# Scores of two heads as 64-row products, one copy of q, the second element's block means moved, and the first unit's q and k loaded in runs of tokens

## The chip, the cores and the metric

The kernel runs on one core of a Trainium2 chip. The metric is the device time of the whole program in microseconds, as a median of several runs. Five engines work side by side: TensorE (PE in the profile, with its weight loads as PEld), VectorE (DVE), ScalarE (ACT), GpSimd (POOL) and SyncE (SP), which issues all the DMA transfers here.

## The reference

The kernel computes an attention over 4 batch elements, 8 heads, 768 positions and 64 columns, and behind it a feed-forward part with weights 512 x 2048 and 2048 x 512. A query sees the keys that lie less than 16 positions away, and besides one summary key for each block of 32 positions (their maximum, column by column) with the mean of the block's values.

```python
k_sum = k.reshape(B, H, nb, block, D).max(axis=3)
v_sum = v.reshape(B, H, nb, block, D).mean(axis=3)
scores_l = scale * np.matmul(q, k.transpose(0, 1, 3, 2))
mask_l = np.abs(pos[:, None] - pos[None, :]) < window
scores_s = scale * np.einsum('bhsd,bhnd->bhsn', q, k_sum)
scores_s = scores_s + np.log(block)
...
a = np.exp(scores_all)
a = a / (np.sum(a, axis=-1, keepdims=True) + 1e-09)
return np.matmul(a, v_all).astype(np.float32)
...
h = x @ w_in
g = h - np.tanh(h)
return (g @ w_out).astype(np.float32)
```

All of it is in float32.

## The kernel before

The work is cut into 8 units, two halves of 384 tokens for each batch element. A unit has 4 pairs of heads, so there are 32 pairs in all; two pairs form a group with common loads. For a pair the steps are: the turns of q and k (`prep`: heads' columns onto partitions, 64 for each head of the pair), copies of them to SBUF (`q high`, `k high`), the block maxima put beside the keys (`top put`), the scores (`score`), the softmax (`min`, `exp`, `sum guard`, `inverse`, `normal`), the turns of the probabilities (`p turn`, `p out`) and the values (`value`). After its four pairs a unit goes through the feed-forward part, 16 chunks `f` of 128 hidden columns each, with products `in`, a pointwise part and products `out`.

A score product covers 64 queries of one head and 118 keys (94 neighbours and 24 block maxima). Its q operand has 128 rows, of which the other head's 64 are zeros; `qf` therefore holds two copies of q, one for each head, and `zeros` fills the unused halves once. Four products, 2 heads x 2 halves of the queries, make one tile of 128 queries, and 3 tiles a pair. The halves go to partitions 0 to 63 and 64 to 127 of a PSUM bank. From the second unit on, the scores of a pair are issued as one task behind the values of the pair before (`scores_and_values`).

Maxima and means of the blocks for the first two batch elements come from loads of their own (`load_part`, then `top_pair` for k and `sum_pair` and `place_v` for v); those for the third and fourth are made later by VectorE and GpSimd. The tables `TOPS` and `SUMS` say in which slot `j` of the program a pair's maxima and sums stand; the loads go into rings of buffers (`gt`, `gu`, `gv`, `gh`, `gl`) that the feed-forward part uses afterwards. The mean of a group is put into the value operand by two transfers (`put_mean`), issued after the sums.

The weights come in 32 loads of 512 KB (`convert`) through a ring of 3 buffers (`wraw`) and are rebuilt by ScalarE and VectorE (`w scale`, `w shift`, `w low`, `w sign`). The first unit's feed-forward part runs while they arrive, with whole float32 products; each weight is split into a high and a low part behind its first use, and later units use three products of these parts.

The order of the program isn't the order of the code. Every step is a task with a cost, and a planner (`Plan.schedule`) simulates the engines, gives each free engine the ready task with the highest level, and emits the tasks in that order. A level is the longest chain behind a task plus two table entries, `BIAS` (for one task) and `KB` (for a kind in a phase); `SL` says how long a step that two engines can do waits for its first engine. A change of any cost, table or dependency can move instructions anywhere. While TensorE has nothing to do in the first part, the planner fills in products on the identity (`keep_warm`), whose outputs nobody reads.

Every operation is issued through one helper, so that the profile gives one line, L72, for nearly all instructions; the tiles tell them apart. `pS`, `pX`, `pY` and `pH` are PSUM banks, `rawq`, `rawk` and `vw` the loaded rows, `wf` a whole weight, `wh` and `wl` its high and low part.

Of the kernel before, what the change touches and what calls it, by code (L numbers as in the profile page):

```python
# [10 lines left out]
F32 = mybir.dt.float32  # L11
# [13 lines left out]

PLAIN = 3
# [11 lines left out]

PREP = [0, 2, 6, 11]

TOPS = {0: [(0, 0)], 1: [(0, 2)], 3: [(0, 1)], 5: [(0, 3)], 9: [(1, 3)], 11: [(1, 2)], 13: [(1, 0)], 15: [(1, 1)]}
SUMS = {0: [(0, 0)], 1: [(0, 1), (1, 1)], 8: [(0, 2)], 9: [(0, 3)], 10: [(1, 0)], 11: [(1, 2)], 13: [(1, 3)]}

SIGNED = set()
# [60 lines left out]
class Plan:  # L105
# [56 lines left out]
    def schedule(self, idle):  # L162
# [49 lines left out]
        while total:  # L212
# [20 lines left out]
            if e == PE and idle is not None:  # L233
                cost, go = idle
                if now > free[PE]:
                    free[PE] = max(free[PE], min(now, getattr(tasks[0], "out", now) + self.SEEN[POOL]))
                while free[PE] < WARM and now - free[PE] > 2 * cost + 0.1:
                    d = Task()
                    d.after, d.order, d.behind = tasks[:1], (), ()
                    d.start, d.engine, d.go = free[PE], PE, go  # L240
                    d.out = free[PE] = clock.run(free[PE], cost)
                    done.append(d)
                now = max(now, free[PE])
# [57 lines left out]
def program(  # L301
# [129 lines left out]
    ident, mask, blk, ga, small = (made[n,] for n in ("ident", "mask", "blk", "ga", "small"))  # L431
# [65 lines left out]
    for j in range(2):  # L497
        zeros(j)
# [839 lines left out]
```

## Time and profile before

| | |
|---|---|
| median of the runs | 727.91 us (725.0 to 730.04) |
| the profiled execution | 722.92 us |
| its span | 721.2 us |
| mean granted TensorE clock | 0.991 |
| HBM read and written | 96.21 MB and 23.07 MB |

The profiled execution's own time is 1.7 us longer than the span between its first and last instruction, and 5.0 us shorter than the median. In a row of the profile "x24" is a number of instructions; a float32 product, other than a transpose, counts twice there, since it is carried out as two instructions. The mean of one instruction is longer than the distance from one to the next, because products overlap; a group's cost is therefore read from the start of the group to the start of what follows it.

### The profile page before, as it was taken

The numbers are of one execution on the slowest core, as the hardware profiler recorded it, in microseconds if no ns is written. First come the engines' busy times: TensorE is split into PE (matmuls) and PEld (weight loads), VectorE is DVE, ScalarE is ACT, GpSimd is POOL, SyncE is SP. The second block draws the span as 40 slices with busy tenths as digits, with TensorE's granted clock in tenths as the row PEclk, the third lists the DMA queues.
The fourth block names the chain that finished last, engine by engine and source line by source line (L and its number), as shares of the span: only waits on it lengthen the run. The fifth ranks groups of instructions, "written<-read, shape, count | busy, mean of one in ns | idle before, by whom it ended". The sixth has DMA issues, their size and how long they took to land.

```text
span 721.2 us, 14213 instructions
## 1 busy us (share of the span) xinstructions
PE 688.8 (96%) x4787; PEld 572.6 (79%) x4787; DVE 431.6 (60%) x1180; ACT 482.3 (67%) x1411; POOL 256.4 (36%) x394
## 2 busy tenths in 40 slices
PE   6898799999999998999999999999999999999995
PEld 5685455558888787889988878998998888999884
DVE  4567878986996645654766557554568533444241
ACT  3467577767789776775897577555669965334981
POOL 3011421131246617422457563433345531111440
PEclk9999899999999999999999999999999999999998
DMA  9989968965665677567465557566544323444101
GB/s 211 234 239 239 307 197 225 281 200 151 202 171 166 179 238 206 138 196 190 123 182 170 164 136 225 142 180 177 170 146 147 119 87 115 147 162 145 45 1 50
DMA packets 158002, 122.67 MB, mean 170 GB/s; under 512 B 94816, under 2 KB 123744, under 8 KB 157920
## 3 DMA queue, kind: packets, MB, share of 16 engines
q1 hardware_dynamic: 157920, 121.67, 58.4%
q8 instruction: 40, 0.66, 0.4%
q14 instruction: 42, 0.34, 0.1%
HBM read 96.21 MB, written 23.07 MB: 165 GB/s over the span
## 4 chain that ended last, share of the span: by engine, by line
PE 77%; DMA 9%; ACT 5%; DVE 3%; SPq 3%; POOL 2%; issue 1%; POOLq 0%; ACTq 0%; DVEq 0%
PE pY L72 34%; PE pH L72 31%; PE pS L72 7%; PE pX L72 5%; SPq L72 3%; DMA wraw<-in_moe_w_in_dram 2%; DMA wraw<-scr 1%; POOL gh L72 1%; ACT prob L72 1%; ACT gu L72 1%; DMA wraw<-in_moe_w_out_dram 1%; DMA gh<-in_v_dram 1%; ACT tmp L72 1%; DVE wf L72 1%; DVE tmp L72 1%
## 5 line engine op out<-in xcount | busy, mean ns | idle before, releaser
L72 PE MATMUL pY<-wf,gh 128*128 128x512 f32 x432 | 178.9, 443 | 5.2 <-POOL gh L72 5.2
L72 PE MATMUL pH<-wh,wraw 128*128 128x384 f32 x672 | 175.3, 342 | 1.3 <-DMA wraw<-scr 1.3
L72 PE MATMUL pY<-wh,gh 128*128 128x512 f32 x336 | 139.4, 415 | 0.0
L72 PE MATMUL pY<-wh,gl 128*128 128x512 f32 x336 | 132.8, 395 | 0.0
L72 PEld LDWEIGHTS pH<-wh,wraw 128*128 128x128 f32 x672 | 120.2, 188 | 9.6 <-DMA wraw<-scr 1.5
L72 POOL TENSOR_TENSOR gu<-gu,gt 128x384 f32<-128x384 f32 x59 | 61.4, 1041 | 185.8 <-ACT gu L72 161.5
L72 ACT ACTIVATE prob<-prob,stat 128x118 f32<-128x118 f32 x248 | 92.3, 384 | 21.3 <-DVE stat L72 20.9
L72 PEld LDWEIGHTS pY<-wf,gh 128*128 128x128 f32 x432 | 80.6, 190 | 30.4 <-issue 12.7
L72 PE MATMUL pH<-wf,wraw 128*128 128x384 f32 x309 | 104.1, 337 | 0.0
L72 PEld LDWEIGHTS pY<-wh,gl 128*128 128x128 f32 x336 | 63.2, 188 | 14.8
L72 PEld LDWEIGHTS pY<-wh,gh 128*128 128x128 f32 x336 | 63.4, 189 | 12.1 <-issue 2.3
L72 ACT ACTIVATE gu<-gu 128x384 f32<-128x384 f32 x128 | 66.9, 523 | 2.2
L72 PE MATMUL pH<-o,wf 128*128 128x384 f32 x188 | 65.3, 446 | 1.6 <-DVE wf L72 1.6
L72 PEld LDWEIGHTS pH<-wf,wraw 128*128 128x128 f32 x309 | 58.0, 188 | 0.0
L72 ACT ACTIVATE gh<-gu 128x384 fp32r<-128x384 f32 x67 | 34.8, 522 | 30.9 <-PE pY L72 21.6
L72 DVE COPY gv<-pH 128x384 f32<-128x384 f32 x50 | 27.9, 558 | 42.4 <-PE pH L72 42.4
L72 DVE CUSTOM_DVE_ANT_0 prob<-pS,mask 128x118 f32<-128x118 f32 x180 | 40.7, 273 | 20.7 <-PE pS L72 20.6
L72 PEld LDWEIGHTS pH<-o,wf 128*128 128x128 f32 x188 | 35.7, 193 | 20.5 <-issue 4.4
L72 ACT ACTIVATE gt<-gu 128x384 f32<-128x384 f32 x42 | 21.9, 523 | 37.1 <-DVE gu L72 36.9
L72 DVE TENSOR_TENSOR gl<-gu,gh 128x384 fp32r<-128x384 f32 x38 | 22.7, 596 | 39.6 <-ACT gh L72 35.7
L72 POOL TENSOR_TENSOR gl<-gu,gh 128x384 fp32r<-128x384 f32 x32 | 33.6, 1055 | 29.4 <-ACT gh L72 27.7
L72 POOL TENSOR_TENSOR gh<-gu,gt 128x384 f32<-128x384 f32 x15 | 23.3, 1555 | 57.3 <-ACT gu L72 33.9
(212 smaller groups left out, 1298.2 us busy)
## 6 DMA issues: line engine op xcount, KB each, us to landing
wraw<-scr SPq DMA_DIRECT2D x75, 512.0 KB
wraw<-in_moe_w_in_dram SPq DMA_DIRECT2D x16, 512.0 KB
wraw<-in_moe_w_out_dram SPq DMA_DIRECT2D x16, 512.0 KB
scr<-wraw SPq DMA_DIRECT2D x16, 512.0 KB
rawq<-in_q_dram SPq DMA_DIRECT2D x48, 128.0 KB
out_dram<-tmp SPq DMA_DIRECT2D x24, 256.0 KB
wraw<-scr SPq DMA_DIRECT2D x21, 256.0 KB
rawk<-in_k_dram SPq DMA_DIRECT2D x32, 128.0 KB
```

The lines of the kernel that those rows point to most:

```text
L72: return lambda *args, **kwargs: self._tc.keep_in_program_order(op(*args, **kwargs))
```

## The change

**Scores.** A product now has only the 64 rows of its head: head 0 uses rows 0 to 63 of `qf` and `kf`, head 1 rows 64 to 127. `qf` holds one copy of q, made by one copy of 128 rows; the zero fills are gone. The heads alternate in the innermost loop, and each head has a bank of its own for its three tiles.

**The second element's maxima and means.** They leave `TOPS` and `SUMS`. Their 16 loads stand in slots 16 and 26 now, into the places of the split weights `wh22` to `wh29`, and the sums, mean turns and maxima in slots 22 to 31, where the first unit's feed-forward part has begun.

**Runs of tokens.** For the first unit a partition of `rawq` takes 3 neighbouring tokens and one of `rawk` 4, in one transfer each and one of a single row, and the turns are products on the identity that write every third or fourth column. The v loads for the sums take 6 tokens of one head in each partition instead of 3 of two heads; the block matrix `blk` becomes 6 x 24 wide and lies in a weight's place. A sum has all 6 products of one head and then all 6 of the other.

**The planner.** `BIAS`, `KB` and `SL` have new numbers throughout, several costs are changed, and a filler product is followed by a pause of 0.1. The tables are left out here.

```diff
+RUNS = 1
+
...
-TOPS = {0: [(0, 0)], 1: [(0, 2)], 3: [(0, 1)], 5: [(0, 3)], 9: [(1, 3)], 11: [(1, 2)], 13: [(1, 0)], 15: [(1, 1)]}
-SUMS = {0: [(0, 0)], 1: [(0, 1), (1, 1)], 8: [(0, 2)], 9: [(0, 3)], 10: [(1, 0)], 11: [(1, 2)], 13: [(1, 3)]}
+TOPS = {0: [(0, 0)], 1: [(0, 2)], 3: [(0, 1)], 5: [(0, 3)]}
+SUMS = {0: [(0, 0)], 1: [(0, 1)], 8: [(0, 2)], 9: [(0, 3)]}
...
-                    d.out = free[PE] = clock.run(free[PE], cost)
+                    d.out = clock.run(free[PE], cost)
+                    free[PE] = d.out + 0.1
...
-    fixed(("blk",), [P, 3, NBH])
+    buf(("blk",), f"wh{2 * NF - 2}", [P, 6, NB])
...
-        buf(("qf", j), f"q{j}", [P, 2, U])
+        buf(("qf", j), f"q{j}", [P, 2 if j else 1, U])
...
-    RAWK = [(("rawk",), i) for i in range(4)]
+    RAWK = [(("rawk",), i) for i in range(5)]
...
+    def in_runs(u):
+
+        return u < RUNS
+
+    def by_runs(x, n):
+        return x.rearrange("p i h d -> p (i h d)").rearrange("p (h t d) -> p h t d", h=HG, t=n)
...
-    def zeros(j):
-        for a in range(2):
...
-            do("const", POOL, 0.75, lambda a=a, o=o: gpsimd.memset(at(("qf", j))[o:o + 64, a], 0.0), w=[(("qf", j), "zero%d" % a)])
-
-    for j in range(2):
-        zeros(j)
-    do("const", DVE, 0.2, lambda: vector.memset(rawk[0:79, 0], 0.0), w=[RAWK[0]])
-    do("const", DVE, 0.2, lambda: vector.memset(rawk[96:P, 3], 0.0), w=[RAWK[3]])
+    do("const", DVE, 0.6, lambda: vector.memset(rawk[0:32], 0.0), w=RAWK)
+    do("const", DVE, 0.6, lambda: vector.memset(rawk[96:P], 0.0), w=RAWK)
...
-                sync.dma_start(st.rearrange("r (a t d) -> r a t d", a=2, t=3), v[b, hs, ts].rearrange("a (r t) d -> r a t d", t=3))
+                sync.dma_start(st, v[b, 2 * p + h].rearrange("(r t) d -> r (t d)", t=6))
...
-            for h in range(2):
-                st = at(("v", b, p, h)).rearrange("r (a t d) -> r a t d", a=2, t=3)
-                for t in range(3):
-                    for a in range(2):
-                        tensor.matmul(at(ps)[D * a:D * (a + 1), NBH * h:NBH * (h + 1)], st[:, a, t], blk[:, t], start=t == 0, stop=t == 2)
...
+            for a in range(2):
+                st = at(("v", b, p, a)).rearrange("r (t d) -> r t d", t=6)
+                for t in range(6):
+                    tensor.matmul(at(ps)[D * a:D * (a + 1), :NB], st[:, t], at(("blk",))[:, t], start=t == 0, stop=t == 5)
...
+        def runs(keys, r0, r1, c0, c1):
+            n, s0 = c1 - c0, t0 - 79 + 4 * r0 + c0
+            src = k[b, hs, s0:s0 + (r1 - r0) * n].rearrange("h (r t) d -> r h (t d)", t=n)
...
+        if in_runs(u):
+            if u % 2 == 0:
+                runs(RAWK[:4], 20, 120, 0, 4)
+                runs(RAWK[4:], 19, 20, 3, 4)
+            else:
+                runs(RAWK[:4], 16, 115, 0, 4)
+                runs(RAWK[4:], 115, 116, 0, 3)
+            src = q[b, hs, t0:t0 + U].rearrange("h (r t) d -> r h (t d)", t=NT)
+            dma("q load", lambda: sync.dma_start(by_runs(rawq, NT).rearrange("r h t d -> r h (t d)"), src), P * HG * D * 4 * NT, 4 * D * NT, w=RAWQ)
+            return
...
+            if in_runs(u):
+                for t in range(n):
+                    for a in range(2):
+                        tensor.matmul(at(ps)[D * a:D * (a + 1), :P * n].rearrange("p (r t) -> p t r", t=n)[:, t], by_runs(raw, n)[:, hs.start + a, t], ident, start=True, stop=True)
+                return
...
-        do("q turn", PE, 0.285, lambda: transposes(pq, rawq, NT), r=[*RAWQ, IDENT], w=[(pq, 0)])
...
-        for a in range(2):
-            rows = slice(64 * a, 64 * a + 64)
-            either("q high", {ACT: 0.42, DVE: 0.5}, lambda e, a=a, rows=rows: copy(e, at(qf)[rows, a], at(pq)[rows, :U], -1.0 / math.sqrt(D)), r=[(pq, 0)], w=[(qf, a)])
+        do("q turn", PE, 0.68 if in_runs(u) else 0.285, lambda: transposes(pq, rawq, NT), r=[*RAWQ, IDENT], w=[(pq, 0)])
+        do("k turn", PE, 0.9 if in_runs(u) else 0.395, lambda: transposes(pk, rawk, 4), r=[*RAWK, IDENT], w=[(pk, 0)])
...
+        either("q high", {ACT: 0.42, DVE: 0.5}, lambda e: copy(e, at(qf)[:, 0], at(pq)[:, :U], -1.0 / math.sqrt(D)), r=[(pq, 0)], w=[(qf, 0)])
...
-        return [(("qf", n), x) for x in (0, 1, "zero0", "zero1")] + [(("kf", n), x) for x in (0, "sums0", "sums1")]
...
-    def score_of(u, p, i):
-        return ("s", u, p, i // 2), 2 * N2 * (i % 2)
+        return [(("qf", n), 0)] + [(("kf", n), x) for x in (0, "sums0", "sums1")]
...
+    def score_of(u, p, i, a):
+        return ("s", u, p, a), N2 * i
...
         for i in range(NT):
-            s, c = score_of(u, p, i)
-            for a in range(2):
-                for half in range(2):
+            for half in range(2):
+                for a in range(2):
+                    s, c = score_of(u, p, i, a)
                     k0 = KS * i + 64 + 64 * half
-                    tensor.matmul(at(s)[64 * half:64 * half + 64, c + N2 * a:c + N2 * (a + 1)], at(qf)[:, a, P * i + 64 * half:P * i + 64 * half + 64], at(kf)[:, k0:k0 + N2], start=True, stop=True)
+                    rows = slice(64 * a, 64 * a + 64)
+                    tensor.matmul(at(s)[64 * half:64 * half + 64, c:c + N2], at(qf)[rows, 0, P * i + 64 * half:P * i + 64 * half + 64], at(kf)[rows, k0:k0 + N2], start=True, stop=True)
...
-            place_v(1, (j - 23) // 8, "pS1")
+        if B > 1 and j in (16, 26):
+            for n, (kind, p1, h) in enumerate((kind, p1, h) for kind in "vk" for p1 in range(2) for h in range(2)):
+                load_part(kind, 1, p1 + (j - 16) // 5, h, f"wh{22 + n}")
+        if B > 1 and 22 <= j < 32 and (j - 22) % 6 < 4:
+            g, n = divmod(j - 22, 6)
+            if n < 2:
+                sum_pair(1, PG * g + n, "pH")
+                if n == 1:
+                    place_v(1, g, "pS1")
+            else:
+                top_pair(1, PG * g + n - 2, "pH")
```

What the change moves is seen in the order of instructions. A row stands for neighbouring instructions that read alike; names are those above, with a buffer's number behind them where there are several, and the sizes are the transfer's, or the product's weight columns and moving columns.

SyncE at the start of the program, before:

```order
L72 DMA gt<-in_k_dram 128x3x128 x2
L72 DMA rawk<-in_k_dram 128x4x64
L72 DMA rawq<-in_q_dram 128x4x64 x2
L72 DMA rawk<-in_k_dram 49x4x64
L72 DMA rawk<-in_k_dram 128x4x64
L72 DMA rawk<-in_k_dram 96x4x64
L72 DMA rawq<-in_q_dram 128x4x64
L72 DMA gv<-in_k_dram 128x3x128
L72 DMA gu<-in_v_dram 128x2x192 x2
```

Seven transfers bring the first group's q and k, with 64 elements a run. The same place now:

```order
L74 DMA gt<-in_k_dram 128x3x128 x2
L74 DMA gv<-in_k_dram 128x3x128
L74 DMA rawq<-in_q_dram 128x4x192
L74 DMA rawk<-in_k_dram 1x4x64
L74 DMA rawk<-in_k_dram 100x4x256
L74 DMA gu<-in_v_dram 128x384 x2
L74 DMA gu<-in_k_dram 128x3x128
L74 DMA gh<-in_v_dram 128x384
```

Three transfers do it, with 192 and 256 elements a run, and the v loads have 384 in one run.

SyncE around the second mean put of the first unit's second group (`vw<-mean`) and the weight loads (`wraw<-in_moe`), before:

```order
L72 DMA vw<-in_v_dram 96x4x64
L72 DMA vw<-mean 24x3x256
L72 DMA rawq<-in_q_dram 128x4x64
L72 DMA vw<-in_v_dram 64x4x64
L72 DMA rawq<-in_q_dram 128x4x64 x2
L72 DMA wraw<-in_moe_w_in_dram 128x4x256
L72 DMA wraw<-in_moe_w_out_dram 128x1024
L72 DMA wraw<-in_moe_w_in_dram 128x4x256
L72 DMA rawk<-in_k_dram 64x4x64
```

All loads for the second element's means are ahead of this place but one. Now:

```order
L74 DMA wh_581<-in_v_dram 128x384
L74 DMA wh_588<-in_v_dram 128x384
L74 DMA wh_597<-in_k_dram 128x3x128
L74 DMA wh_604<-in_k_dram 128x3x128
L74 DMA vw<-mean 24x3x256 x2
L74 DMA wh_627<-in_v_dram 128x384
L74 DMA wraw<-in_moe_w_in_dram 128x4x256
L74 DMA wraw<-in_moe_w_out_dram 128x1024
L74 DMA wraw<-in_moe_w_in_dram 128x4x256
L74 DMA rawq<-in_q_dram 128x4x64 x2
```

Those loads (`wh`) stand among the weights now; eight of the sixteen come behind these rows.

TensorE in the first unit's feed-forward part, around the scores of a pair of the second unit, before:

```order
L72 MATMUL pS_68<-ident,prob 118x128 x2
L72 MATMUL pH<-o_448,wf_1079 128x384
L72 MATMUL pH<-o_453,wf_1079 128x384
L72 MATMUL pH<-o_766,wf_1079 128x384
L72 MATMUL pH<-o_811,wf_1079 128x384
L72 MATMUL pX<-probT,vw 64x64 x12
L72 MATMUL pS_1138<-k_254,q_138 64x118 x8
L72 MATMUL pS_68<-k_254,q_138 64x118 x4
L72 MATMUL pH<-o_448,wf_1155 128x384
```

Values, then scores: eight products into one bank, four into the other. Now, with the sum of one pair of the second element (`pH<-wh_123`, where `wh_123` is the block matrix) ahead of it:

```order
L74 MATMUL pH<-o_697,wf_1094 128x384
L74 MATMUL pH<-wh_123,wh_811 64x24 x6
L74 MATMUL pH<-wh_123,wh_892 64x24 x6
L74 MATMUL pX<-probT,vw 64x64 x12
L74 MATMUL pS_1180<-k_287,q_254 64x118
L74 MATMUL pS_68<-k_287,q_254 64x118
...
L74 MATMUL pH<-o_406,wf_1193 128x384
```

The scores go to the two banks in turn, and a sum of the second element stands between the feed-forward products.

More of the change, by code (lines that the diff above doesn't have):

```diff
@@ L430, in program @@
     fixed(("small",), [P, 1])
-    ident, mask, blk, ga, small = (made[n,] for n in ("ident", "mask", "blk", "ga", "small"))
+    ident, mask, ga, small = (made[n,] for n in ("ident", "mask", "ga", "small"))
     def make_ident():
@@ L461, in program @@
     do("const", POOL, 2.3, make_mask, w=[MASK])
-    do("const", POOL, 0.7, make_blk, w=[BLK])
+    do("const", POOL, 1.2, make_blk, w=[BLK])
     do("const", DVE, 0.05, lambda: vector.memset(ga, GA), w=[GAK])
@@ L636, in load_part @@
     def load_part(kind, b, p, h, tag):
-        base = buf((kind, b, p, h), tag, [P, U], F32, RINGS[tag])
-        hs, ts = slice(2 * p, 2 * p + 2), slice(U * h, U * (h + 1))
+        base = buf((kind, b, p, h), tag, [P, U], F32, RINGS.get(tag, 1))
         def load():
@@ L657, in top_pair @@
                    r=[(st[a], 0)] if a else (), w=[(st[0], 0)])
-        do("top turn", PE, 0.325, lambda: [tensor.transpose(at(ps)[:, P * c:P * (c + 1)], at(st[0])[:, P * c:P * (c + 1)], ident) for c in range(3)],
+        do("top turn", PE, 0.42, lambda: [tensor.transpose(at(ps)[:, P * c:P * (c + 1)], at(st[0])[:, P * c:P * (c + 1)], ident) for c in range(3)],
            r=[(st[0], 0), IDENT], w=[(ps, 0)])
@@ L686, in go @@
                 tensor.matmul(at(ps)[:NB, P * pr:P * (pr + 1)], at(x)[:, pr], ident, start=True, stop=True)
-        do("mean turn", PE, 0.5, go, r=[(x, pr) for pr in range(PG)] + [IDENT], w=[(ps, 0)])
+        do("mean turn", PE, 0.55, go, r=[(x, pr) for pr in range(PG)] + [IDENT], w=[(ps, 0)])
         do("mean out", ACT, 0.28, lambda: scalar.activation(mean[32 * g:32 * g + NB], at(ps)[:NB, :HG * D], AF.Copy), r=[(ps, 0)], w=[MEAN[g]])
@@ L735, in go @@
                 tensor.matmul(at(ps)[:NB, D * hh:D * (hh + 1)], ident[:96, NB * hh:NB * (hh + 1)], at(acc)[:96], start=True, stop=True)
-        do("mean turn", PE, 0.44, go, r=[(acc, 0), IDENT], w=[(ps, 0)])
+        do("mean turn", PE, 0.55, go, r=[(acc, 0), IDENT], w=[(ps, 0)])
         do("mean out", ACT, 0.28, lambda: scalar.activation(mean[32 * g:32 * g + NB], at(ps)[:NB, :HG * D], AF.Copy, scale=1.0 / 32), r=[(ps, 0)], w=[MEAN[g]])
@@ L849, in scores_and_values @@
     def scores_and_values(now, before, tags, px_tag):
-        r, w, cost, parts = [], [], 0.25, []
+        r, w, cost, parts = [], [], 0.13, []
         if before is not None:
             px = bank(("px", *before), px_tag)
-            r, w, cost = r + value_keys(*before), w + [(px, i) for i in range(NT)], cost + 0.75
+            r, w, cost = r + value_keys(*before), w + [(px, i) for i in range(NT)], cost + 0.72
             parts.append(lambda: value(*before))
@@ L857, in scores_and_values @@
             banks = [bank(("s", u, p, n), tag) for n, tag in enumerate(tags)]
-            r, w, cost = r + score_keys(u, p), w + [(x, n) for x in banks for n in range(4)], cost + 1.23
+            r, w, cost = r + score_keys(u, p), w + [(x, n) for x in banks for n in range(NT)], cost + 0.6
             parts.append(lambda: score(*now))
@@ L865, in first @@
         def first(i, a):
[L866 to L867 removed]
+            s, c = score_of(u, p, i, a)
             m = 1 if u % 2 == 0 and i == 0 else 2 if u % 2 == 1 and i == NT - 1 else 0
@@ L887, in softmax @@
         for i, a in both:
-            s, _ = score_of(u, p, i)
-            do("min", DVE, 0.21, lambda i=i, a=a: first(i, a), r=[(s, 2 * (i % 2) + a), MASK], w=[(("pr", u, p, i), a), (st, 2 * i + a)])
+            s, _ = score_of(u, p, i, a)
+            do("min", DVE, 0.21, lambda i=i, a=a: first(i, a), r=[(s, i), MASK], w=[(("pr", u, p, i), a), (st, 2 * i + a)])
         for i, a in both:
```

23 lines of the change are left out of this document (10 added, 13 removed).

## The prediction

> **What bounds the kernel now.** I read the page first, for the span and for which engine fills it.
>
> ```profile
> span 721.2 us, 14213 instructions
> PE 688.8 (96%) x4787; PEld 572.6 (79%) x4787; DVE 431.6 (60%) x1180; ACT 482.3 (67%) x1411; POOL 256.4 (36%) x394
> ```
>
> TensorE is busy for 96% of the span, but a mean hides stages. So I asked next for busy time by stage (columns: stretch, its length, busy time of PE, PEld, DVE, ACT and POOL, granted TensorE clock, DMA share, GB/s).
>
> ```profile
> 0.00:50.00 50.00, 40.51 (x526) 35.51 (x527) 28.08 (x111) 22.87 (x84) 9.53 (x40) 1.00 0.89 217
> 50.00:100.00 50.00, 43.96 (x240) 25.61 (x239) 36.91 (x83) 32.69 (x90) 13.04 (x11) 0.93 0.88 252
> 100.00:150.00 50.00, 47.84 (x242) 26.61 (x241) 45.97 (x107) 36.67 (x102) 11.86 (x11) 1.00 0.92 264
> 150.00:721.00 571.00, 556.46 (x3784) 484.88 (x3782) 320.69 (x881) 390.05 (x1137) 221.97 (x333) 0.99 0.51 151
> L72 PE MATMUL pS<-ident 128*128 128x128 f32 x116 | 17.2, 297 | 0.5 <-DVE q L72 0.3
> ```
>
> There are two regimes. Up to about 150 us the DMA engines are 88 to 92% taken; in the first 50 us, 17.2 of TensorE's 40.51 us are filler products on the identity (last row). From 150 us on TensorE is busy in 556.46 of 571 us, and 8.3 us of the rest come after its last product, which ends at 712.92 (in the next fence): there an instruction taken off TensorE shortens the span by its time, and nothing else does. The timelines of SyncE and TensorE show the hand-over.
>
> ```profile
> 44.97 1.55 SPq L72 DMA_DIRECT2D vw<-in_v_dram  x1
> 50.25 0.94 PE L72 MATMUL pY<-probT,vw 118*64 118x64 f32 x24
> 52.31 2.75 PE L72 MATMUL pH<-o,wf 128*128 128x384 f32 x8
> 59.39 0.33 SPq L72 DMA_DIRECT2D wraw<-in_moe_w_out_dram  x1
> 149.55 0.34 SPq L72 DMA_DIRECT2D wraw<-in_moe_w_out_dram  x1
> 712.52 0.40 PE L72 MATMUL pY<-wh,gl 128*128 128x512 f32 x1
> ```
>
> The last v rows that the first unit needs are issued at 44.97 us, its last value product runs at 50.25 us, the first MoE product at 52.31 us. The eighth weight load is issued at 59.39 us, the thirty-second and last at 149.55 us.
>
> **The change, part by part. First, the loads.** In the order of SyncE I added up bytes (shape times 4). Before, 10.33 MB have been issued with that last v load; now the last thing that the first unit needs (its second mean put) comes at 8.62 MB, because 1.6 MB of the second element's k and v stand behind it. At the eighth weight load the count falls from 14.57 to 13.01 MB, at the last from 37.05 to 35.73 MB. At the pace of before (14.57 MB in 59.39 us, 0.245 MB/us) 1.56 MB are 6.4 us; 1.32 MB at 37.05/149.55 = 0.248 are 5.3 us. Packets get longer as well: 1.6 MB of q and k come in runs of 768 and 1024 bytes, not 256, and 2.75 MB of v by then in 1536, not 768.
>
> ```profile
> 10.00:20.00 10.00, 8.90 (x129) 7.34 (x129) 6.20 (x32) 5.19 (x23) 1.23 (x4) 1.00 0.90 209
> 70.00:80.00 10.00, 10.00 (x35) 5.59 (x34) 8.87 (x25) 8.47 (x28) 2.77 (x3) 1.00 1.00 343
> ```
>
> The stretch of short packets moved 209 GB/s, one of mostly weights 343. If all 4.35 MB went from the one pace to the other it would save 20.8 - 12.7 = 8.1 us; if run length didn't matter, nothing. The new runs lie nearer the first row; I take 2 us. Together the weights come 8.4 us earlier (5.3 to 14.5). The first MoE product comes 9.7 us earlier, near 43 us (1.71 MB at 10.33 MB/46.5 us = 0.222 MB/us, and the 2 us), which the weights then cut to 8.4.
>
> **The moved step** brings into the weight stage everything that it issues: 16 loads, 4 sums, 4 maxima (a transpose, two maxima over pairs, one reduction each) and 2 mean turns with their copies.
>
> ```profile
> 29.11 0.88 PE L72 MATMUL pY<-blk,gu 128*64 128x12 f32 x24
> 29.91 0.82 PE L72 MATMUL pS<-ident 128*128 128x128 f32 x5
> 35.73 0.55 PE L72 MATMUL pH<-ident,rawq 128*128 128x128 f32 x3
> 36.64 1.43 PE L72 MATMUL pS<-k,q 128*64 128x118 f32 x24
> L72 DVE TENSOR_REDUCE th<-pH 128x24 f32<-128x384 f32 x8 | 4.4, 550 | 1.7 <-PE pH L72 1.7
> L72 DVE TENSOR_TENSOR gt<-gt 128x192 f32<-128x192 f32 x3 | 1.1, 359 | 3.7 <-DMA gt<-in_k_dram 3.7
> ```
>
> A sum takes 29.91 - 29.11 = 0.80 us now. The new one has as many products, twice as wide, and no longer alternates between column halves; no row shows that. Its bounds are 0.80 us and the 1.21 us that 24 products of 118 columns take below; I take 1.2. The 7 transposes between 35.73 and 36.64 take 0.13 us each, so a maximum's 3 take 0.4 us and a mean turn's 4 products 0.5 us: TensorE gets 4 x 1.6 + 1.0 = 7.4 us here, and VectorE 4 x 0.55 + 8 x 0.36 = 5.1 us. What hides TensorE's part is that it idled 100 - 43.96 - 47.84 = 8.2 us between 50 and 150 us, and starts 9.7 us earlier. I cost it at nothing; without that cover it is up to 7.4 us.
>
> **Turns of the first unit.** The q and k turns of a pair take 36.64 - 35.73 = 0.91 us; as 28 half-width products at the scores' 50 ns, scaled from 118 to 128 columns, they take 1.5 us. Four times 0.6 us lie in the start, under waiting loads: nothing, or 2.4 us without them. The same cover hides VectorE's larger fills of rawk. The filler falls from 58 to 23 products in the program (the trace shows each as two); if the clock fell with it, 8 products would cost 3.88 instead of 2.74 us (rows below), again inside waits for loads.
>
> **The scores.** The timelines of TensorE and of its weight loads around one pair in the saturated stage:
>
> ```profile
> 446.20 0.34 PE L72 MATMUL pH<-wf,wraw 128*128 128x384 f32 x1
> 446.47 0.92 PE L72 MATMUL pX<-probT,vw 118*64 118x64 f32 x24
> 447.22 1.38 PE L72 MATMUL pS<-k,q 128*64 128x118 f32 x24
> 448.53 0.50 PE L72 MATMUL pY<-wh,gh 128*128 128x512 f32 x1
> 446.47 0.78 PEld L72 LDWEIGHTS pX<-probT,vw 118*64 118x64 f32 x24 [0.25 <-issue]
> 447.16 1.21 PEld L72 LDWEIGHTS pS<-k,q 128*64 128x64 f32 x24
> ```
>
> The 24 value products take 447.22 - 446.47 = 0.75 us from start to start, the 24 score products 1.21 us. A value product moves 64 columns, a score product 118, and 0.75/1.21 = 0.62 is not 64/118 = 0.54: the short ones already show a little of another floor, 31 ns each. Now two heads use different halves of the array's rows and alternate, and go to different banks. If that doubles the rate, a pair saves 0.61 us; if not, nothing. Nearest is the floor of the value products: 0.75 us, a saving of 0.46. Of 32 pairs 4 lie in the start and 4 in the weight stage, where the saving is covered by waits; 24 x 0.46 = 11.0 us come off the span (0 to 14.6).
>
> One thing speaks against: values and scores shared one shape of tiles, now they don't. The row shows 0.25 us in which the loads of weights waited ahead of the first small tile. At most 24 x 0.25 = 6.0 us are added; I take none, since the product ahead of it runs on until 446.54. The Trainium skill (TensorEngine Tiling (Array Packing), Key Properties) says that a change of tiling mode drains TensorE; by that rule up to 6.0 us would be added and the forecast below would be 714, while no row of before shows a change between two small shapes.
>
> **One copy of q** takes one 64-row copy away per pair, and the zero fills at the start:
>
> ```profile
> L72 DVE TENSOR_SCALAR q<-pS 64x384 f32<-64x384 f32 x22 | 12.1, 552 | 5.1 <-PE pS L72 4.4 <-ACT q L72 0.3
> L72 POOL MEMSET q<- 64x384 f32 x4 | 1.6, 412 | 0.1
> ```
>
> That is 0.55 us of VectorE or ScalarE for each of 32 pairs, neither of which bounds the long stage: nothing.
>
> **The sum**: 722.92 us (the profiled execution) - 8.4 - 11.0 = 703.5 us. The median shown, 727.91, is 5.0 us above that execution, so I forecast 708.5, say 709 us.
>
> **The rivals.** *Both parts pay in full.* The scores halve, and a stall of before is not repeated:
>
> ```profile
> 80.16 5.23 POOL L72 TENSOR_TENSOR gh<-gu,gt 128x384 f32<-128x384 f32 x1 [1.58 <-ACT gu L72]
> L72 POOL TENSOR_TENSOR gu<-gu,gt 128x384 f32<-128x384 f32 x59 | 61.4, 1041 | 185.8 <-ACT gu L72 161.5
> L72 DVE TENSOR_TENSOR gu<-gu,gt 128x384 f32<-128x384 f32 x11 | 7.9, 719 | 11.6 <-ACT gu L72 10.7 <-ACT gt L72 0.9
> 85.45 2.07 PE L72 MATMUL pY<-wf,gh 128*128 128x512 f32 x2 [3.87 <-POOL gh L72]
> 88.17 3.88 PE L72 MATMUL pH<-o,wf 128*128 128x384 f32 x8
> ```
>
> A GpSimd product took 5.23 us where others of its size take about 1.04; TensorE waited 3.87 us, and its next 8 products took 3.88 us at a lower clock where 2.75 is usual (52.31), 5.0 us in all. The order now gives GpSimd 11 of the first unit's 16 such products, not 15, so it may go; another may come. 722.9 - 8.4 - 14.6 - 5.0 = 694.9, or 700 us. Chance 0.18.
>
> *The scores keep their 1.21 us,* because 24 loads of weights and not the streaming bound them. For it: the value products' floor. Against: their 24 loads took 0.78 us, so loads can go faster. Then 722.9 - 8.4 = 714.5, or 719.5 us. Chance 0.13. The Trainium skill (TensorE: Matmul & The Clock Gate, LDWEIGHTS (loading the stationary operand)) gives columns divided by 1.2 in ns, 53 ns for 64 columns, 1.28 us for 24; by that rule it would be this rival. The row's 0.78/24 = 32 ns disagrees, and the row decides.
>
> *VectorE becomes the bound of the weight stage.* It was busy 45.97 of 50 us in the third stretch, and converts every weight. It gets 5.1 us, and 4 more MoE products of 0.72 us (5 of 16 instead of 1), and loses at most 2.2 us of q copies: 5.7 us more, which eat the head start down to 2.7: 722.9 - 2.7 - 11.0 = 709.2, or 714 us. Against it: 50 - 36.91 = 13 us are free in the second stretch. Chance 0.14.
>
> *Slower: alternating by rows breaks the overlap that is there.* Today neighbours differ in the column half, and the 1.21 us are half of what 24 products would take one after another. In the new order neighbours share the column half and differ in rows; if those don't run together a pair costs 2.42 us, 24 x 1.21 = 29 us more: 722.9 - 8.4 + 29.0 = 743.5, or 748 us. It decides from 8.4/24 = 0.35 us more per pair, that is above 1.56 us. Nothing in the trace shows row halves at work, so it can't be excluded. Chance 0.06.
>
> **Chances and range.** The forecast itself (703 to 715 us) gets 0.49. One per cent is 7.3 us, about what the three runs spread over (725.0 to 730.04) lets a measurement tell. Faster by more, below 720.6 us: the first, third and forecast cases and over half of the second, less a margin for a new stall from the changed order of the whole program: 0.84. Same 0.10, slower 0.06. The range reaches from a little below the full-pay case to just past the unhelped scores with one new 5 us stall: 697 to 724.
>
> **What would show it.** Right: the first pH<-o,wf product near 43 us, the eighth weight load near 51 and the last near 141 us; score groups of 24 products in about 0.75 us start to start, with the gap ahead of the next full product unchanged; TensorE as full after 150 us as now. Wrong: 1.21 us or more per score group, or a gap between the value and the score products; VectorE above 46 of 50 us with TensorE waiting for wf; a GpSimd product of several us ahead of a TensorE wait.

## The result, and the profile after

The changed kernel takes 707.69 us (median of 4 runs, 706.07 to 708.68) where the kernel before takes 728.97 beside it (4 runs, 725.0 to 733.34): a ratio of 0.9705, 95% interval 0.9644 to 0.9765. Run again in a later comparison it took 707.66 us (6 runs) against 722.69 (11 runs), 0.9809, interval 0.9761 to 0.9858. Over all the comparisons below the changed kernel has a median of 707.7 us (10 runs, 704.57 to 710.91) and the kernel before 725.2 (57 runs, 715.99 to 733.34). Side by side the medians differ by 21.3 and by 15.0 us, over all runs by 17.5: nearer to 2.4% than to the 3% of the first comparison. The ratios and intervals leave out runs that lie more than 1.5% above the fastest run of their kernel, medians and ranges hold all runs, so the two can differ.

The page of the changed kernel's profiled execution (708.19 us), span and engines:

```profile
span 706.4 us, 14180 instructions
...
PE 678.0 (96%) x4801; PEld 558.8 (79%) x4801; DVE 408.9 (58%) x1125; ACT 489.7 (69%) x1434; POOL 250.6 (35%) x390
```

Its busy time by stage, in the columns used before (stretch, length, PE, PEld, DVE, ACT, POOL, granted clock, DMA share, GB/s):

```profile
0.00:50.00 50.00, 39.29 (x506) 32.98 (x507) 26.87 (x110) 24.63 (x88) 5.48 (x28) 1.00 0.82 216
50.00:100.00 50.00, 48.54 (x293) 28.76 (x292) 43.66 (x97) 34.75 (x95) 7.87 (x9) 0.97 0.88 259
100.00:150.00 50.00, 50.00 (x255) 27.52 (x253) 44.93 (x102) 39.19 (x111) 10.36 (x15) 1.00 0.93 280
150.00:706.00 556.00, 540.21 (x3754) 469.53 (x3752) 293.43 (x820) 391.12 (x1145) 226.93 (x338) 0.99 0.52 153
```

Profile against profile, the gain is 722.92 - 708.19 = 14.7 us. The 8.2 us that TensorE idled between 50 and 150 us are down to 1.5, and from 150 us on it is busy for 540.21 us instead of 556.46. The timelines of SyncE, ScalarE and TensorE at the places that the prediction named:

```profile
37.46 0.95 SPq L74 DMA_DIRECT2D wh<-in_v_dram  x2
37.49 0.37 ACT L74 ACTIVATE mean<-pY 24x256 f32<-24x256 f32 x1
38.46 0.96 SPq L74 DMA_DIRECT2D wh<-in_k_dram  x2
39.52 1.75 SPq L74 DMA_DIRECT2D vw<-mean  x2
43.95 0.92 PE L74 MATMUL pX<-probT,vw 118*64 118x64 f32 x24 [2.31 <-DMA vw<-mean]
46.84 2.75 PE L74 MATMUL pH<-o,wf 128*128 128x384 f32 x8
52.27 4.54 PE L74 MATMUL pH<-o,wf 128*128 128x384 f32 x8 [1.39 <-ACT gu L74]
54.92 0.33 SPq L74 DMA_DIRECT2D wraw<-in_moe_w_out_dram  x1
140.27 0.35 SPq L74 DMA_DIRECT2D wraw<-in_moe_w_out_dram  x1
```

The first MoE product comes at 46.84 us (5.5 earlier than before), the eighth weight load at 54.92 (4.5 earlier), the last at 140.27 (9.3 earlier). The mean is written by 37.86 us, but its two transfers stand behind four early loads of the second element and are issued at 39.52; the first unit's values wait 2.31 us for them.

TensorE and its weight loads around one pair in the full stage:

```profile
403.56 0.92 PE L74 MATMUL pX<-probT,vw 118*64 118x64 f32 x24
404.41 0.84 PE L74 MATMUL pS<-k,q 64*64 64x118 f32 x24
405.18 0.50 PE L74 MATMUL pY<-wh,gh 128*128 128x512 f32 x1
403.56 0.78 PEld L74 LDWEIGHTS pX<-probT,vw 118*64 118x64 f32 x24 [0.25 <-issue]
404.41 0.61 PEld L74 LDWEIGHTS pS<-k,q 64*64 64x64 f32 x24
```

From the scores' start to the next full product it is 0.77 us, 1.31 before (448.53 - 447.22 in the prediction's rows). From the values' start to the scores' it is 0.85, 0.75 before. A pair went from 2.06 to 1.62 us. In the medians over 23 and 21 such places the four numbers are the same.

Waits of TensorE (what for, us in total, how many, the longest):

```profile
PE pH L74 <- DMA wraw<-scr: 3.7, 5, 1.4
...
PE pX L74 <- DMA vw<-mean: 2.3, 1, 2.3
...
PE pH L74 <- ACT gu L74: 1.4, 1, 1.4
```

Those for `wraw<-scr` lie behind 150 us, and so do smaller ones for `stat` and `prob`. I also added up, from 150 us to the last product's start, the distance from each group's start to the next one's; that sum fell from 562.5 to 548.7 us. Scores: 31.5 to 20.4. What is left of the first unit's whole MoE products (`pH<-o,wf` in groups of eight, and `pY<-wf,gh` in groups of two to six): 13.6 to 4.0. Values: 18.8 to 22.2. Turns of the probabilities, with their waits: 11.9 to 15.1. Products with the sums of weights, with their waits: 120.7 to 122.9. So 20.7 us were won at the two places that the prediction named and 8.8 given back at three others; the rest is spread over the other groups.

### The profile page after: what moved, and what is told of

Read it like the earlier page. It is cut to its first block, busy times and chain, and to the rows that moved or that the text cites. A ratio compares the mean times of both kernels' runs of the same rounds, so it can differ in the third digit from the quotient of the medians.

```text
span 706.4 us, 14180 instructions
## 1 busy us (share of the span) xinstructions
PE 678.0 (96%) x4801; PEld 558.8 (79%) x4801; DVE 408.9 (58%) x1125; ACT 489.7 (69%) x1434; POOL 250.6 (35%) x390
## 5 line engine op out<-in xcount | busy, mean ns | idle before, releaser
L74 PE MATMUL pY<-wh,gh 128*128 128x512 f32 (+1 forms) x348 | 139.7, 406 | 0.0
L74 POOL TENSOR_TENSOR gu<-gu,gt 128x384 f32<-128x384 f32 x52 | 53.5, 1029 | 158.5 <-ACT gu L74 131.7
L74 ACT ACTIVATE prob<-prob,stat 128x118 f32<-128x118 f32 x232 | 86.9, 384 | 13.2 <-DVE stat L74 11.6
L74 PEld LDWEIGHTS pY<-wh,gh 128*128 128x128 f32 (+1 forms) x348 | 63.9, 186 | 11.4 <-issue 1.9
L74 ACT ACTIVATE gu<-pH 128x384 f32<-128x384 f32 x65 | 31.7, 488 | 37.1 <-PE pH L74 33.6
L74 ACT ACTIVATE gv<-pH 128x384 f32<-128x384 f32 x60 | 29.2, 487 | 33.7 <-PE pH L74 33.3
L74 PEld LDWEIGHTS pH<-o,wf 128*128 128x128 f32 x188 | 35.8, 193 | 20.4 <-issue 4.5
L74 POOL COPY k<-th 64x72 f32<-64x72 f32 (+1 forms) x37 | 9.9, 266 | 97.9 <-PE pS L74 73.4
L74 POOL TENSOR_TENSOR prob<-prob,stat 128x118 f32<-128x118 f32 x75 | 35.1, 481 | 24.5 <-DVE stat L74 18.6
L74 DVE TENSOR_TENSOR gl<-gu,gh 128x384 fp32r<-128x384 f32 x41 | 25.2, 614 | 31.6 <-ACT gh L74 29.2
L74 POOL TENSOR_TENSOR gl<-gu,gh 128x384 fp32r<-128x384 f32 x29 | 31.5, 1086 | 18.0 <-ACT gh L74 12.7
```

The lines of the kernel that those rows point to most:

```text
L74: return lambda *args, **kwargs: self._tc.keep_in_program_order(op(*args, **kwargs))
```

## The experiments

The theory is the prediction's: the start gives 8.4 us (6.4 of them by bytes, 2 by longer runs), the scores give 11.0, the copy of q and the moved step count nothing. Each kernel was timed beside the kernel before on its chip; the changed kernel itself ran beside `two_copies`, `short_pieces` and `mean_first`. The edits below are against the changed kernel, or against the kernel before where the name begins with it.

### The scores alone, both ways

`rows128`: the products have 128 rows again.

```diff
-tensor.matmul(..., at(qf)[rows, 0, ...], at(kf)[rows, k0:k0 + N2], ...)
+tensor.matmul(..., at(qf)[:, 0, ...], at(kf)[:, k0:k0 + N2], ...)
```

> The changed kernel with each score product over all 128 rows of q and k again (both heads' rows are summed, so the scores are not the reference's); order, banks, copies and loads as changed. If the score term is what I took it for: a group of 24 score products takes 1.2 us again instead of 0.77, the values ahead of it 0.75 instead of 0.85, so a pair costs 2.06 instead of 1.62 us, 24 pairs in the full stage 10.6 us, and the time is 717 to 720 us. If the score products are covered by something else, it stays at 706 to 709.

`heads_outer`: the loops over heads and halves change places.

```diff
-            for half in range(2):
-                for a in range(2):
+            for a in range(2):
+                for half in range(2):
```

> The changed kernel with the two inner score loops swapped: heads outside, halves inside, so that neighbours differ in the column half as before the change, and every third product in the rows. If any two of the four tiles overlap whatever their order, the group keeps its 0.77 us and the time 706 to 709. If only the rows of direct neighbours overlap beside columns of the ones after, the group goes back towards 1.2 us and the time to 717 to 720.

`before_rows64`: the kernel before with products of 64 rows and a bank for each head; the planner keeps the bank names that it had, so that the order stays, and some softmax minima can be read from the wrong tile.

```diff
-            for a in range(2):
-                for half in range(2):
...
-                    tensor.matmul(..., at(qf)[:, a, ...], at(kf)[:, k0:k0 + N2], ...)
+            for half in range(2):
+                for a in range(2):
...
+                    tensor.matmul(..., at(qf)[rows, a, ...], at(kf)[rows, k0:k0 + N2], ...)
```

> The kernel before with only the score products changed to 64 rows, heads alternating and a bank for each head; its order, its two copies of q, its loads and moved steps stay. My theory (the score term counts alone, in the full stage): 24 x 0.44 = 10.6 us off, ratio 0.985, 716 to 720 us. Rival (the order written for the old costs gives it away in other waits): 726 to 730.

Measured: `rows128` 718.24 us (10 runs, 715.47 to 720.13), `heads_outer` 707.14 (4 runs, 704.25 to 708.7), `before_rows64` 715.45 (10 runs, 705.92 to 724.92), the kernel before 723.9 (19 runs). The ratios are 0.9943 (0.9905 to 0.9981), 0.9787 (0.9708 to 0.9866) and 0.9843 (0.9783 to 0.9903). The 64 rows are worth 718.24 - 707.14 = 11.1 us in the new order. In the old one, where the runs scatter more, the medians give 8.5 us and the ratio 11.4. Which half alternates makes no difference.

One pair of `rows128` on TensorE's timeline:

```profile
394.89 0.92 PE L74 MATMUL pX<-probT,vw 118*64 118x64 f32 x24
395.64 1.43 PE L74 MATMUL pS<-k,q 128*64 128x118 f32 x24
397.00 0.50 PE L74 MATMUL pY<-wh,gh 128*128 128x512 f32 x1
```

Its busy time from 150 us on:

```profile
150.00:713.00 563.00, 550.65 (x3749) 483.46 (x3748) 290.29 (x817) 391.29 (x1142) 227.22 (x338) 0.99 0.50 150
```

And one pair of `before_rows64`, with its busy time from 150 us on:

```profile
396.56 0.92 PE L72 MATMUL pX<-probT,vw 118*64 118x64 f32 x24
397.41 0.84 PE L72 MATMUL pS<-k,q 64*64 64x118 f32 x24
398.17 0.50 PE L72 MATMUL pY<-wh,gh 128*128 128x512 f32 x1
...
150.00:710.00 560.00, 545.39 (x3776) 470.92 (x3774) 319.73 (x877) 387.65 (x1135) 225.65 (x333) 1.00 0.50 153
```

With 128 rows TensorE is busy for 550.65 us from 150 us on, 10.4 more than in the changed kernel; `before_rows64` has 545.39, 11.1 less than the kernel before. With 128 rows the values take 0.75 us again (395.64 - 394.89), with 64 rows 0.85 in the old program as well. So the 0.10 us come with the change between two small shapes of tiles, in either program: 24 x 0.10 = 2.4 us. The prediction bounded it at 0.25 a pair and took none. The Trainium skill (TensorEngine Tiling (Array Packing), Key Properties) says that a change of tiling mode drains TensorE; the rows agree that it costs, and put it at 0.10 us here.

### The loads

`after_small`: the second element's 16 moved loads are cut to a sixth, and GpSimd fills the rest with zeros; `before_small` is the same in the kernel before.

```diff
+            if b == 1:
+                gpsimd.memset(st[:, D:], 0.0)
+                sync.dma_start(st[:, :D], v[0, 2 * p, 0:P])
-            if kind == "v":
+            elif kind == "v":
```

> The changed kernel with the 16 moved loads of the second element cut to a sixth of their bytes, the rest of each buffer filled with zeros by GpSimd (wrong sums for that element). If the weight stage is still paced by the loads, as I predicted, 2.6 MB less at 0.25 MB/us let it end up to 10 us earlier: 698 to 703 us. Rival: TensorE, busy for 50.00 of 50 us there, now paces it: at most 3 us, 704 to 708.

> The kernel before with the sixteen loads of the second element's early k and v cut to a sixth (2.6 MB less; GpSimd fills the rest with zeros, so the second element's maxima and means are of other data). Theory (the prediction's: the bytes ahead of the first unit's last v rows set the start): first MoE product 7 to 11 us earlier than the 52.31 us of before, last weight load as much, time 7 to 11 us below the kernel before. Rival (as in the changed kernel, where the same cut was worth 3 us): 0 to 4 us below it.

`loads_added`: eight more loads ahead of the v loads of the first unit's second half, into weight buffers that are filled later.

```diff
+            if small_only and (kind, n) == ("k", 19):
+                for j in range(8):
+                    sync.dma_start(at(("wf", wholes[20 + j]))[:, :U]..., k[1, j]...)
```

> The changed kernel with eight more loads (1.57 MB of k, into weight buffers that are filled only later) issued in one go ahead of the nine v loads that the first unit's second half needs; nothing is taken away. By that the first unit has as many bytes ahead of its end as before the change, and the last weight load too. Theory (the prediction's main term: the transfers pace the start, 1.57 MB at 0.222 to 0.248 MB/us): first MoE product and eighth weight load 6 to 7 us later than the changed kernel's (46.4 to 46.8 and 54.5 to 54.9), last weight load 5 us later or more, time 5 to 7 us above the changed kernel's 707.4. Rival (TensorE and VectorE pace the weight stage now and bring the later loads in): the first product is later by as much, but by the last weight load at most 2 us of it are left, and the time is 0 to 2 us above.

`short_pieces`: the run lengths of before, everything else as changed.

```diff
-                sync.dma_start(st, v[b, 2 * p + h].rearrange("(r t) d -> r (t d)", t=6))
+                sync.dma_start(st.rearrange("r (a e) -> r a e", a=2), v[b, 2 * p + h].rearrange("(a r t) d -> r a (t d)", a=2, t=3))
...
+                src = k[b, hs].rearrange("h s d -> (h s) d").rearrange("(j s) d -> s j d", j=16)[r0:r1]
...
-            src = q[b, hs, t0:t0 + U].rearrange("h (r t) d -> r h (t d)", t=NT)
...
+            src = q[b, hs].rearrange("h s d -> (h s) d").rearrange("(j s) d -> s j d", j=12)[:P]
...
```

> The changed kernel with the first unit's q and k loads cut into 256-byte pieces and the loads for the sums of v into 768-byte pieces, as they were before the change: same transfers in number, order and bytes, other tokens in them (so these queries, keys and sums are of the wrong tokens). Theory (the prediction's term of 2 us for longer runs, bounds 0 to 8.1): the first third of the start gets slower, the third weight load is issued 1 to 3 us later and the time is 1 to 3 us above the changed kernel beside it. Rival (the head start came from the 1.7 MB moved behind it alone, and the weight stage is now paced by TensorE): within 0.7 us of it.

The yardstick for `short_pieces`, and for `two_copies` and `mean_first` further down, is the changed kernel on the same chip:

> The changed kernel once more, as the yardstick of the three kernels that run beside it on the same chip. If the profile of the kernel before (span 721.2 us, below all of its timed runs) was a fast draw and the changed kernel scatters little, this gives 705 to 709 us again, some 18 to 21 us below the kernel before. If the first comparison was a lucky draw of the changed kernel, it gives 711 us or more.

Measured: `after_small` 704.76 us (4 runs; `heads_outer`, which does the changed kernel's work, has 707.14 beside it). `before_small` 718.84 (12 runs; kernel before 725.83, 23 runs; ratio 0.9911, 0.9872 to 0.9951). `loads_added` 712.89 (6 runs, 709.66 to 715.19; 0.9845, 0.98 to 0.989). `short_pieces` 709.9 (6 runs, 707.95 to 711.06) beside `after_again` at 707.66 (6 runs, 704.57 to 710.91). SyncE and TensorE in `loads_added`:

```profile
31.58 7.97 SPq L74 DMA_DIRECT2D wf<-in_k_dram  x8
50.89 1.55 PE L74 MATMUL pX<-probT,vw 118*64 118x64 f32 x24 [1.28 <-DMA vw<-mean]
56.02 3.50 PE L74 MATMUL pH<-o,wf 128*128 128x384 f32 x8
61.77 0.37 SPq L74 DMA_DIRECT2D wraw<-in_moe_w_out_dram  x1
147.06 0.35 SPq L74 DMA_DIRECT2D wraw<-in_moe_w_out_dram  x1
```

In the changed kernel more bytes do move the start, as the theory has it. 1.57 MB more ahead of the first unit's end move the values that wait for the mean by 6.9 us (50.89 against 43.95), the eighth weight load by 6.9 and the last by 6.8. The first product moves by 9.2 us, more than expected; the rest of it goes with the clock, for these values took 1.55 us instead of 0.92, at a granted clock of 0.69 between 40 and 50 us and 0.62 in the 10 us behind. The kernel's time is 5.2 us above the 707.7 of the other comparisons; by the ratios to the kernel before (0.9845 against 0.9809) it would be 2.6.

Cutting the second element's loads by 2.6 MB is worth 7.0 us in the kernel before, at the lower end of what was expected, but not in the way that was expected. One line of `before_small`:

```profile
50.44 5.33 PE L72 MATMUL pH<-o,wf 128*128 128x384 f32 x16
```

Its first MoE product comes 1.9 us earlier than the 52.31 us of before, not 7 to 11, and `before_one_copy`, which has all the loads, has it at 50.55 us. So this run doesn't show that the bytes set the start of the kernel before. In the changed kernel, where part of these loads stand behind the first unit, the same cut gives 2.4 us: nearer the rival.

`short_pieces` is 2.2 us above the changed kernel, the prediction's 2 for the runs of tokens, but the two kernels' ranges overlap, and its trace doesn't show the slower start:

```profile
10.00:20.00 10.00, 9.89 (x121) 9.07 (x122) 4.86 (x24) 3.90 (x17) 0.24 (x1) 1.00 0.90 208
...
41.76 0.46 SPq L74 DMA_DIRECT2D wraw<-in_moe_w_in_dram  x1
45.79 2.75 PE L74 MATMUL pH<-o,wf 128*128 128x384 f32 x8
```

From 10 to 20 us the short pieces moved 208 GB/s, where the changed kernel moved 187 in its first profile and 162 in its second (`after_again`). The third weight load is issued at 41.76 us (41.87 and 41.99 in those two), and the first MoE product comes at 45.79 us, earlier than their 46.84 and 46.42. That longer runs shorten the start is therefore not shown, and where the 2.2 us arise stays open.

### The copy of q

`two_copies`: each pair's copy is issued as two copies of 64 partitions; `two_copies_first` does it in the first unit only (`if u == 0`).

```diff
-lambda e: copy(e, at(qf)[:, 0], at(pq)[:, :U], ...)
+lambda e: [copy(e, at(qf)[64 * a:64 * a + 64, 0], at(pq)[64 * a:64 * a + 64, :U], ...) for a in range(2)]
```

> The changed kernel with the copy of q issued as two copies of 64 partitions each, as before the change; nothing else moves. That is 24 more copies of about 0.47 us on ScalarE or VectorE, 11 us of busy time. Theory (the prediction's step: one copy of q is worth nothing): within 1 us of the changed kernel beside it, and no new TensorE wait for q of over 1 us in sum. Rival: the copies of a pair's q stand in front of its scores and of the turns' eviction on ScalarE, so each pair of the 24 pays 0.1 to 0.47 us: 2 to 11 us slower.

> The changed kernel with two copies of q in the six pairs of the first unit only, which are prepared before the first MoE product; the other eighteen pairs keep one. Two copies in all 24 pairs cost 3.7 us. Theory (ScalarE and VectorE are in the way at the start, where TensorE waits for the scores of the pair at hand): most of it is here, 2 to 4 us above the changed kernel's 707.4. Rival (each copy delays its pair alike, or the copies that stand among the weights' conversions do it): 0 to 1 us above.

`before_one_copy`: the kernel before without the second copy.

```diff
...
-lambda e, a=a, rows=rows: copy(e, at(qf)[rows, a], at(pq)[rows, :U], ...)
+lambda e, a=a: a or copy(e, at(qf)[:, 0], at(pq)[:, :U], ...)
```

> The kernel before with the second of the two copies of q left out in every pair (the first takes all 128 partitions, the second half is zero throughout, so the second head's scores are of zeros); products, loads and order stay. Theory (the prediction: nothing): within 1 us of the kernel before. Rival (what the two copies in the changed kernel cost, 3.7 us, they cost before as well): 2 to 5 us below it.

(The program has 32 pairs and so 32 copies, four of them in the first unit, not the 24 and six that the expectations speak of.)

Measured: `two_copies` 711.39 us (6 runs, 709.57 to 712.63), 3.7 above the changed kernel beside it; `two_copies_first` 708.57 (6 runs, 705.77 to 710.28), about 1 above the 707.7 of other comparisons, with no changed kernel beside it; `before_one_copy` 722.28 (12 runs; kernel before 725.83; 0.9947, 0.9916 to 0.9979), 3.6 below. The prediction's "nothing" is wrong, both ways by the same size. How much of it the first unit holds these times can't tell, since by the ratios (0.9785 and 0.9809) `two_copies_first` would even be the faster. Two stretches of `two_copies`, by the table of busy times:

```profile
50.00:60.00 10.00, 7.05 (x36) 4.27 (x35) 5.59 (x10) 4.34 (x10) 1.30 (x1) 0.73 0.81 216
...
150.00:710.00 560.00, 546.05 (x3771) 471.86 (x3769) 300.16 (x826) 406.75 (x1176) 227.31 (x339) 0.99 0.51 154
```

Its second group of MoE products and its last weight load on the timelines, and below them the last weight load of `two_copies_first`:

```profile
55.61 5.49 PE L74 MATMUL pH<-o,wf 128*128 128x384 f32 x8 [2.95 <-ACT gu L74]
145.14 0.34 SPq L74 DMA_DIRECT2D wraw<-in_moe_w_out_dram  x1
...
140.41 0.34 SPq L74 DMA_DIRECT2D wraw<-in_moe_w_out_dram  x1
```

The second of those stretches in `after_again`:

```profile
150.00:705.00 555.00, 539.79 (x3749) 469.34 (x3748) 289.45 (x817) 389.98 (x1142) 226.52 (x338) 0.99 0.51 152
```

And its rows on the timelines:

```profile
51.86 2.85 PE L74 MATMUL pH<-o,wf 128*128 128x384 f32 x8 [1.39 <-ACT gu L74]
138.17 0.35 SPq L74 DMA_DIRECT2D wraw<-in_moe_w_out_dram  x1
```

TensorE has 6.3 us more to do after 150 us (546.05 against 539.79), which is work that the start and the weight stage didn't get to: the head start is smaller. So the price lies before 150 us, although ScalarE is busy for 16.8 us more after it. With two copies in the first unit only, the last weight load is issued at 140.41 us, as in the changed kernel (140.27 and 138.17), with two everywhere at 145.14: most of what this execution lost came with the later units' copies, which are made while the weights arrive. Between 50 and 60 us TensorE waited 2.95 us for ScalarE instead of 1.39, and at a granted clock of 0.73 its next 8 products took 5.49 us. How much of this one execution is the copies and how much the clock, it doesn't tell; the medians say 3.7 us for both together.

### An attempt at a better version

`mean_first`: the two mean transfers that TensorE waits for go ahead of the four loads that stand in front of them; nothing else moves. The edit is in the planner's last step, which sorts the tasks into their order.

```diff
...
+            loads = [t for t in done[:first] if t.engine == SP][-4:]
...
+                part = done[n:second + 1]
+                done[n:second + 1] = [t for t in part if t not in loads] + loads
```

> The changed kernel with two mean copies of the first unit's second half issued ahead of the four early loads of the second element that stand in front of them, and nothing else moved. In the changed kernel the mean copies are issued at 39.52 us, 1.66 us after the mean is written at 37.86, and the value products wait 2.31 us for them. Theory (TensorE paces the start and the weight stage now, so an earlier first MoE product is time won): that wait falls by 1 to 1.7 us, the first MoE product comes 1 to 1.7 us earlier and the time is 0.7 to 1.7 us below the changed kernel beside it. Rival (the maxima of the four later loads come later by as much, and the stage after them waits instead, or DMA volume sets the weight stage): within 0.6 us or above it.

Measured: 710.07 us (6 runs, 707.0 to 710.62), 2.4 above the changed kernel beside it, with ranges that overlap, so no gain. Its timelines:

```profile
38.39 1.76 SPq L74 DMA_DIRECT2D vw<-mean  x2
42.09 0.92 PE L74 MATMUL pX<-probT,vw 118*64 118x64 f32 x24
44.66 0.36 DVE L74 TENSOR_TENSOR wh<-wh 128x192 f32<-128x192 f32 x1 [3.05 <-DMA wh<-in_k_dram]
44.98 1.46 PE L74 MATMUL pH<-o,wf 128*128 128x384 f32 x4
47.00 0.75 DVE L74 TENSOR_TENSOR wh<-wh 128x192 f32<-128x192 f32 x2 [1.98 <-DMA wh<-in_k_dram]
47.67 0.55 DVE L74 COPY o<-pX 128x384 f32<-128x384 f32 x1
48.27 0.91 PE L74 MATMUL pH<-o,wf 128*128 128x384 f32 x2 [1.84 <-DVE o L74]
49.93 1.38 PE L74 MATMUL pH<-o,wf 128*128 128x384 f32 x2 [0.75 <-ACT o L74]
```

And a stretch of its busy times:

```profile
50.00:55.00 5.00, 5.00 (x29) 3.32 (x30) 4.86 (x9) 3.72 (x9) 0.42 (x1) 0.52 0.94 231
```

The wait for the mean is gone and the first MoE product comes 1.9 us earlier than in the changed kernel's first profile, but a new wait takes its place. In VectorE's order the copy `o<-pX` stands behind the second element's maxima, and these wait for the loads that are now later (3.05 and 1.98 us); the copy starts at 47.67 us, and TensorE waits 1.84 us for that copy in the middle of its first products, and 0.75 for the next. Right after, its clock is 0.52 for 5 us.

## Why the prediction was right, and where it wasn't

The forecast was 709 us (697 to 724), the measurement 707.69; not every step behind it held, and that the number was hit so closely is luck.

**The scores: right in mechanism, and in size by two errors.** 11.0 us were predicted, 11.1 measured in the new order. Row halves run side by side: the 24 loads of weights took 0.61 us, 25 ns each, less than the 31 ns that I called a floor, so the scores gave more (24 x 0.54 = 13.0 by the rows) and the change of shape took 2.4 back. The step "I take none" failed; that the larger gain covered it is luck. (The 1.21 us from which I took the saving are the time of the weight loads; from start to start the 24 products took 1.31, by the rows above that sentence.) The rival in which alternating by rows breaks the overlap, and the one in which the loads of weights keep 1.21 us, are both out by the 0.77 us.

**The head start: too large, and right at its end by luck.** The last weight load came 9.3 us earlier (8.4 predicted), but the first MoE product 5.5 instead of 9.7 and the eighth weight load 4.5 instead of 8.4. I took the bytes ahead of the second mean transfer at before's pace, 0.222 MB/us. The 8.62 MB were out at 41.27 us, 0.209 MB/us. A stretch of the changed kernel at the start, beside the 209 GB/s and 0.90 of before:

```profile
10.00:20.00 10.00, 8.89 (x107) 8.24 (x109) 3.94 (x20) 3.15 (x14) 0.24 (x1) 1.00 0.76 187
```

Longer runs did not fill the DMA engines better here. Nor is it the smaller number of transfers: `short_pieces`, with as many transfers, has 0.90 and 208 GB/s in this stretch, and the second execution of the changed kernel 0.62 and 162. What sets the pace there stays open.

Between the eighth and the last weight load of the kernel before lies the stall of the first rival, 5.0 us around 85.45 us, and 4.5 + 5.0 nearly make the 9.3. I had left it out of the sum, as one that may go while another comes. But it belongs to the old order: in all four of its traces TensorE waits 5.0 to 5.3 us for GpSimd between 50 and 150 us, and in none of the ten traces of the new order does it wait for GpSimd there. In `before_one_copy` the wait ends at 142.78 us, behind the last weight load:

```profile
139.19 0.35 SPq L72 DMA_DIRECT2D wraw<-in_moe_w_out_dram  x1
...
PE pY L72 <- POOL gh L72: 5.0, 1, 5.0
```

There this load is as early as in the changed kernel, with all of the old loads in front of it. So the last weight load doesn't show the 8.4 us; the eighth, ahead of the stall, shows 4.5. No run took the stall away alone.

**The copy of q: wrong.** "Nothing" was 3.6 to 3.7 us. The step that failed is the choice of stage: "neither of which bounds the long stage" is true, but the copies of the first units are made before it, where ScalarE and VectorE also convert the weights.

**The moved step at nothing: not settled.** `before_rows64` and `heads_outer`, timed beside each other, differ in all but the 64 rows: 8.3 us by the medians, 4.0 by the ratios, and 5.2 us of TensorE's work after 150 us (545.39, and 540.21 in the changed kernel). The forecast gave the loads alone 8.4 us. But 3.6 of these 4 to 8 us are the copy of q, and the missing stall is in them too. So the loads brought less than I took, or the moved step and the new order took some of it back. TensorE has no time to spare for that step: a sum takes 1.31 us (58.05 - 56.74 in the changed kernel; I took 1.2), and the idle time that was to hide it was mostly the stall, 5.2 of 8.2 us. The parts measured one at a time give 11.1 + 3.7 + 2.2 + 5.2 = 22.2 us, with the doubts on the last two, and the whole 17.5 over all runs. The 4.7 us between them can be the moved step, the new order of the program (the 5.4 us that the turns and the products with the weights' sums gave back would fit) or parts that don't add up, since several act on one stage; none of these was run alone. TensorE as full after 150 us as before is nearly right: it idles 556 - 540.21 = 15.8 us there, where it idled 571 - 556.46 = 14.5.

**VectorE as the bound: no.** It is busy 44.93 of 50 us in the third stretch, less than before, and TensorE has no idle time there.

**The offset: wrong, and it hid the rest.** I added 5.0 us because the median was that far above the profiled execution. Over 57 runs the kernel before lies between 716 and 733 us with a median of 725.2, 2.3 above that execution, and the changed kernel's profile (708.19) lies at its median. The sum alone said 703.5 us, 4.7 below what that execution took; the two errors are of one size and cancelled in the forecast of 709, by luck.

## What to carry to other kernels

Price an edit in each stage it touches: work that is free beside a full TensorE can be paid for in full where a chain of transfers, conversions and first products is the limit. When a group of small products changes shape, look at the group before it as well, because that is where the change shows. A stall in one profile can belong to the order of the program: look for it in the traces of other variants before it is left out of the sum. And before moving a transfer forward, see what stands in order behind the one that it overtakes.

## What the runs showed that I had not expected

Weight loads of 64 x 64 tiles follow each other at 25 ns (0.61 us for 24), those of 118 x 64 at 32 ns (0.78 for 24), those of 128 x 64 ahead of products of 118 columns at 50 ns (1.21 for 24, the prediction's row). All have 64 columns, so these alone don't set the pace. And it makes no difference whether a product's neighbour lies in the other half of the rows or of the columns (`heads_outer`).

TensorE's granted clock fell after waits of 1.4 to 3 us in the weight stage, though not every time: the same wait of 1.39 us was followed by 8 products in 4.54 us in one execution of the changed kernel and in 2.85 in another, and in `before_one_copy` a wait of 2.02 us by 8 in 2.82. In `mean_first`, waits of 1.84 and 0.75 us went ahead of a clock of 0.52. The Trainium skill (TensorE: Matmul & The Clock Gate, HAM oscillation) tells of idle gaps above about 3.4 us; the rows here show it after shorter ones.

The scatter goes with the old order more than with its products. In one comparison the kernel before ran from 715.99 to 729.93 us and the changed one from 704.57 to 710.91; `before_rows64`, with the new products in the old order, spread over 19 us, and `rows128`, the old products in the new order, over 4.7. But `before_one_copy`, in the old order, spread over only 6.7 us. What causes it wasn't tried.
